# First MLP in blocks of 288 and 432 columns, with six weight chunks streamed and seven more attention slots

## Chip, cores and metric

One core of one Trainium2 chip. The metric is the device time of one execution of the whole program, in microseconds (us). The kernel before took 1003.7 us (median of 3 runs, 1002.4 to 1004.23).

## The reference, cut to what matters

```python
def phi(x):                       # x: 4 batches, 8 heads, 576 positions, 64 deep
    proj = einsum('bhsd,df->bhsf', x, w_phi)          # 128 features
    proj = proj - max(abs(proj), axis=-1)
    return concatenate([exp(proj), exp(-proj)], -1)   # 256
q_p, k_p = phi(q), phi(k)
kv  = einsum('bhsf,bhsd->bhfd', k_p, v);  z = sum(k_p, axis=2)
x   = einsum('bhsf,bhfd->bhsd', q_p, kv) / (einsum('bhsf,bhf->bhs', q_p, z) + 1e-6)
x   = x as (2304 tokens, 512)
h   = x @ w_in1;  x2 = (h * sigmoid(h)) @ w_out1      # 512 -> 2048 -> 512, first MLP
h   = max(x2 @ w_in2, 0);  out = (h * h) @ w_out2     # second MLP
```

All of it is float32 in and out. The weights of both MLPs are float64 in DRAM.

## The kernel before

**Number format.** A float32 value is split into two float32r values, hi (a cast on ACT) and lo (a subtraction on DVE), and a product is three matmuls: lo x hi, hi x lo, hi x hi. So every operand of PE needs one ACT and one DVE operation first (`hi_act` L355, `lo_on` L358; DVE's subtractions all show as L360, ACT's casts as L356).

**Attention.** There are 4 batches j of 576 tokens; 8 heads are handled in pairs, p = 0 to 3. `keys_of(j, p)` (L621) builds phi(k) and kv for one pair of one batch. `queries_of(b, p)` (L863) handles one *half*: b = 0 to 7, 288 tokens, half b belongs to batch b // 2. It projects the queries (L900, L901), takes the maximum over partitions on GpSimd (L911), makes exponentials, splits them, multiplies by kv (L963) and divides: the denominator row goes to DRAM and back in three small DMAs (rr<-qn L978, rd<-rr L985, qb<-rd L988), because the reciprocal is taken with the row spread over 96 partitions. The product x (L1001, two DVE operations) is split into the x buffer of its half. Attention's tiles live in slots of 128 x 576 float32: 28 early ones for batch 0's keys and half 0, 12 (`NT`) for all else; a unit (one pair) can only be under way if one of `NU` = 4 tokens is free.

**First MLP.** 8 blocks of 288 tokens (half b is block b), each with 16 chunk steps; a step (`chunk`, L1019) handles 128 of the 2048 inner columns: 12 matmuls of 288 columns into a PSUM bank (L1035), tanh and gate on ACT and DVE, split, and 12 matmuls that accumulate into four banks (L1071). The 16 weight chunks (8 KB per partition each, hi and lo of both matrices) are converted from float64 once, during block 0 and before (`w_conv` L454, `w_split` L522), and stay in SBUF: 8 tiles in pool `w`, 8 in `wq`, which opens once the early slots are done. The result of a block goes to DRAM (x2d, L1090). I call the steps by number: step 16 i + c is chunk c of block i, 0 to 127.

**Second MLP.** Its weights are converted in 32 parts while the first MLP runs and stored to DRAM (w2d, L546). Its first matrix is multiplied by a seven-product scheme on 2 x 2 sub-blocks (`x_sums` L1098, `w_sums` L552, `quad` L1167, matmuls L1191), the gated result goes to DRAM in 144 KB pieces (gd, L1250), and its second matrix is multiplied in blocks of 512 columns, the last 256 (`gate_of`, `down`, L1294).

**What sets the order.** All operations are listed with an engine, a cost, a key, reads, writes and buffers. `Plan.run` (L160) simulates the engines: whenever an engine is free it takes the ready operation with the lowest key whose buffers are free. The order found so is emitted as the program; on the chip each engine runs its own list in order and waits on semaphores. Keys are chunk steps: the first MLP's step has its own number, and `want` (L1323) places attention at so many steps ahead (the table `KEYS`, L271). All DMAs are issued by SP, in the planned order; a DMA that waits holds up those behind it. There are 8 PSUM banks: four accumulators, two for L1035, two for attention.

**Lines the change touches.** `KEYS` and the `want` calls (L1332 to L1374), the pools (L293 to L336), `w_tile` (L508), `w_split`, `w_sums`, `x_buf` (L856) and the end of `queries_of` (L996 to L1014), `chunk`, `x_sums`, `quad`, `gate_of`, `down`.

Of the kernel before, what the change touches and what calls it, by code (L numbers as in the profile page):

```python
# [51 lines left out]
class Buf:  # L52


    def __init__(self, pool, make, unit):
        self.pool, self.make, self.unit, self.users, self.tile = pool, make, unit, 0, None
# [10 lines left out]
class Plan:  # L67
# [92 lines left out]
    def run(self):  # L160
# [9 lines left out]
        while left:  # L170
            moved = True
            while moved:
                moved = False
                for e in engines:
# [43 lines left out]
            while events and events[0][0] <= now:  # L218
# [45 lines left out]
def dma(kb):  # L264
# [10 lines left out]
    "nwr": 4, "wsp": -6.82,  # L275
# [4 lines left out]
def attention_then_two_mlps(ctx, tc, kT, qT, v, w_phi, w1, w2, out):  # L280
# [9 lines left out]
    NXT, NGQ = 7, 7  # L290
# [4 lines left out]
    xp = ctx.enter_context(tc.tile_pool(name="xp", bufs=2, side="right"))  # L295
    gp = ctx.enter_context(tc.tile_pool(name="gp", bufs=NG, side="right"))
# [20 lines left out]
    def wide_pool():  # L317
# [7 lines left out]
    gd = tc.dram_tile([128, NC, NTOK], F32, name="gd")  # L325
    rd = tc.dram_tile([2 * B * NP, 2 * HB], F32, name="rd")

    plan = Plan({
        "t": NT, "raw": NRAW, "att": NATT, "h": 2, "acc": 0, "eb": 4, "e": NE, "eunits": NEU, "w": NC - NW, "wq": 0, "x": 2, "kv": NP, "v": 2,
        "g": NG, "o": 2, "xx": 2, "rr": 2, "mx": 4, "units": NU, "c": NCV, "xt": 0, "gq": 0, "pb": 0,  # L330
    })
    wide = [0, {"xt": NXT, "gq": NGQ}]
    plan.last = {
        "eb": [0, {"acc": 4}], "e": [0, {"wq": NW}], "t": wide, "kv": wide, "v": wide,
# [4 lines left out]
    def slot(name, unit, shape=(128, S), dt=F32):  # L339
        if unit.early:  # L340
            return Buf("e", lambda: ep[0].tile(list(shape), dt, tag="t", name=name), unit)
        return Buf("t", lambda: tp.tile(list(shape), dt, tag="t", name=name), unit)

    def bank(name, unit, pool_="att"):
        if pool_ == "att" and unit.early == 2:
            pool_ = "eb"
        return Buf(pool_, lambda: psb.tile([128, 512], F32, tag="b", name=name), unit)

# [105 lines left out]
    def w_conv(layer, c, parts, key):  # L454
# [42 lines left out]
        hold = min(int(key) - 6, NB * NC - 1) if layer else 0  # L497
# [24 lines left out]
    def w_split(layer, c, parts, f, u, key, engine):  # L522
# [28 lines left out]

    def w_sums(q, key):  # L552
        u = plan.unit()
        hi, lo = (w_tile(1, 2 * q + x) for x in range(2))
# [9 lines left out]
        def parts(x):  # L564
            return get((hi, lo)[x]).rearrange("p a n -> p (a n)")[:, :7 * 256].rearrange("p (a n) -> p a n", n=256)

        SPLITS = ((0, 2, 0), (3, 4, 2), (0, 4, 3))

        def split_hi(i):
            a, b, o = SPLITS[i]  # L570
            hi_act(parts(0)[:, o:o + b - a], get(f)[:, a:b])

        def split_lo(i):
            a, b, o = SPLITS[i]
            lo_on("DVE", parts(1)[:, o:o + b - a], get(f)[:, a:b], parts(0)[:, o:o + b - a])
# [19 lines left out]
        op(key, "ACT", act(1024), lambda: split_hi(2), r=[(W, 1)], w=[(W, "hi", 2)], bufs=[f, hi], unit=u)  # L595
        op(key, "DVE", dve(1024), lambda: split_lo(2), r=[(W, 1), (W, "hi", 2)], w=[(W, "lo", 2)],
           bufs=[f, hi, lo], unit=u)

# [257 lines left out]
    def x_buf(u):  # L856
        if u not in xs:
            xs[u] = Buf(
                "x", lambda: [xp.tile([128, ND, HB], F32R, tag=f"x{i}", name=f"x{i}_{u}") for i in range(2)], None
            )  # L860
        return xs[u]

    def queries_of(b, p, key, lo_engine="DVE"):  # L863
# [132 lines left out]
        x = Buf("xx", lambda: sp.tile([128, HB], F32, tag="xx", name="x" + n), None)  # L996
        xb = x_buf(b)
# [15 lines left out]
        op(key, "ACT", act(HB), x_hi, r=[(Q, "x")], w=[("xh", b, p)], bufs=[x, xb])  # L1013
        op(key, "DVE", dve(HB), x_lo, r=[(Q, "x"), ("xh", b, p)], w=[("xl", b, p)], bufs=[x, xb])  # L1014
# [4 lines left out]
    def chunk(i, c, key):  # L1019
        n = f"{i}_{c}"  # L1020
        C = ("c", 0, i, c)
        w = wch[0, c]
        xb = xs[i]
        ps = bank("h" + n, None, "h")
        gb = Buf("g", lambda: [gp.tile([128, HB], dt, tag=t, name=t + n)
                               for t, dt in (("a", F32), ("gh", F32R), ("gl", F32R))], None)

        def gemm1():
# [3 lines left out]
            for cc in range(ND):  # L1032
                f = slice(cc * 128, (cc + 1) * 128)
                for a, x in ((ww[:, 1, f], xh), (ww[:, 0, f], xl), (ww[:, 0, f], xh)):
                    nc.tensor.matmul(get(ps)[:, :HB], a, x[:, cc], start=k == 0, stop=k == 3 * ND - 1)  # L1035
                    k += 1

        def f1():
            nc.scalar.activation(out=get(gb)[0], in_=get(ps)[:, :HB], func=AF.Tanh, scale=0.5)  # L1039

        def f2():
            a = get(gb)[0]
            nc.vector.scalar_tensor_tensor(  # L1043
                out=a, in0=a, scalar=1.0, in1=get(ps)[:, :HB], op0=ALU.add, op1=ALU.mult
            )
# [12 lines left out]
        op(key, "ACT", act(HB), g_hi, r=[(C, "g")], w=[(C, "gh")], bufs=[gb])
        op(key, "DVE", dve(HB), g_lo, r=[(C, "g"), (C, "gh")], w=[(C, "gl")], bufs=[gb])
        W = [(("wf", 0, c, 1), "hi"), (("wf", 0, c, 1), "lo")]  # L1060
        for d in range(ND):
# [4 lines left out]
            def gemm2(d=d, acc=acc):  # L1066
# [8 lines left out]
            op(key + P["g2"], "PE", 3 * MM, gemm2, r=W + [(C, "gh"), (C, "gl")], w=[("acc", i, d)],  # L1075
# [349 lines left out]
```

## Time and profile before

| | |
|---|---|
| runs | 1002.4, 1003.7, 1004.23 us |
| profiled execution | 1002.71 us, span 1000.9 us |
| PE busy | 981.7 us (98%), 6656 matmuls |
| DVE, ACT, GpSimd busy | 677.7, 579.5, 94.6 us |
| mean granted TensorE clock | 0.993 |
| DMA | 126.68 MB, mean 127 GB/s |

The span runs from the first to the last instruction; the rest of the execution's time lies around it. "Granted clock" 1.00 is 2.4 GHz, 0.5 is 1.2 GHz; a value between is a mean over a stretch. Matmuls overlap: the bar of one is longer than the distance to the next, so a count of bars in a window has about two more than the window holds, and a busy PE can still be slower than its best. A row of a view of groups reads: line, engine, operation, tile written <- tiles read, shapes, count | busy us, mean ns of one | idle time of the engine ahead of it, and what ended it.

### The profile page before, as it was taken

To read this page: it belongs to the slowest core of one execution; us is meant where nothing else is said; L and a number is where in the kernel's file an instruction comes from. 1 tells how busy PE (TensorE), PEld (TensorE's weight loads), DVE (VectorE), ACT (ScalarE), POOL (GpSimd) and SP (SyncE) were. 2 spreads that over 40 slices of the span, in tenths; PEclk is the share of its full clock that TensorE was granted. 3 is DMA by queue.
4 is the path that set the end of the run, shared out by engine and by line. 5 is a ranking of instruction groups with operands and counts; after the bars stand their busy time and mean duration, and the time that the engine had idled before them with its cause. 6 is when DMAs were issued, how large, how long until landed. Compare 5 with 4: busy or idle time off the path is not lost.

```text
span 1000.9 us, 17956 instructions
## 1 busy us (share of the span) xinstructions
PE 981.7 (98%) x6656; PEld 920.4 (92%) x6656; DVE 677.7 (68%) x1295; ACT 579.5 (58%) x1385; POOL 94.6 (9%) x68
## 2 busy tenths in 40 slices
PE   9969999999999999999999999999999999999998
PEld 6739999999999999999989999999999988888888
DVE  5999997766557777788898799975767733232321
ACT  6867866776777676776574464564555732222221
POOL 3140003210011300011020002010200000000000
PEclk9979999999999999999999999999999999999999
DMA  9536601231102132454545635443436654343322
GB/s 272 175 118 216 217 27 37 61 87 50 39 25 61 44 104 97 135 174 133 139 137 172 209 120 193 166 155 113 148 108 225 205 184 127 103 128 103 119 66 73
DMA packets 76578, 126.68 MB, mean 127 GB/s; under 512 B 14922, under 2 KB 42186, under 8 KB 74442
## 3 DMA queue, kind: packets, MB, share of 16 engines
q1 hardware_dynamic: 76490, 125.54, 40.0%
q8 instruction: 52, 0.85, 0.4%
q14 instruction: 36, 0.29, 0.1%
HBM read 88.64 MB, written 36.79 MB: 125 GB/s over the span
## 4 chain that ended last, share of the span: by engine, by line
PE 93%; DVE 4%; DMA 1%; issue 1%; ACT 0%; POOL 0%; SPq 0%; DVEq 0%
PE h L1035 20%; PE y L1294 20%; PE o L1071 19%; PE pb L1191 7%; PE pc L1191 5%; PE pa L1191 5%; PE pn L963 5%; PE pk L704 3%; PE pkv L766 3%; PE pkv L812 3%; DVE w L360 1%; PE pq L900 1%; PE pq L901 1%; DVE wc L492 1%; DVE wc L488 1%
## 5 line engine op out<-in xcount | busy, mean ns | idle before, releaser
L1071 PE MATMUL o<-gh,w 128*128 128x288 f32 x1024 | 232.1, 298 | 0.0
L1035 PE MATMUL h<-x,w 128*128 128x288 f32 x1536 | 225.1, 296 | 0.1
L1035 PEld LDWEIGHTS h<-x,w 128*128 128x128 f32 x1536 | 211.4, 188 | 1.0 <-ACT mx L726 0.4
L1294 PE MATMUL y<-g,w 128*128 128x512 f32 (+1 forms) x960 | 201.7, 372 | 0.0
L1294 PEld LDWEIGHTS y<-g,w 128*128 128x128 f32 x960 | 167.5, 188 | 33.6
L1071 PEld LDWEIGHTS o<-gh,w 128*128 128x128 f32 x1024 | 172.7, 188 | 2.6 <-issue 1.9
L1071 PE MATMUL o<-gl,w 128*128 128x288 f32 x512 | 150.4, 294 | 0.0
L360 DVE TENSOR_TENSOR g<-gr,g 128x512 fp32r<-128x512 f32 (+1 forms) x80 | 51.0, 638 | 130.3 <-ACT g L356 130.2
L356 ACT CAST g<-gr 128x512 fp32r<-128x512 f32 (+1 forms) x80 | 45.9, 577 | 137.1 <-PE y L1294 134.7
L1039 ACT ACTIVATE a<-h 128x288 f32<-128x288 f32 x128 | 52.9, 413 | 82.3 <-PE h L1035 81.4
L911 POOL PARTITION_ALL_REDUCE qm<-qp x32 | 73.1, 2310 | 257.9 <-ACT qp L904 238.5
L1071 PEld LDWEIGHTS o<-gl,w 128*128 128x128 f32 x512 | 96.4, 188 | 0.2
L1191 PE MATMUL pb<-xt,w 128*128 128x288 f32 x576 | 88.4, 296 | 0.7 <-DVE glq L1206 0.6
L1043 DVE SCALAR_TENSOR_TENSOR a<-a,h 128x288 f32<-128x288 f32 x128 | 57.5, 450 | 43.7 <-ACT a L1039 42.8
L1191 PEld LDWEIGHTS pb<-xt,w 128*128 128x128 f32 x576 | 80.6, 188 | 1.4 <-DVE glq L1206 0.8
L360 DVE TENSOR_TENSOR gl<-a,gh 128x288 fp32r<-128x288 f32 x128 | 64.2, 502 | 11.8 <-ACT gh L356 10.8
L356 ACT CAST gh<-a 128x288 fp32r<-128x288 f32 x128 | 55.9, 437 | 18.5 <-DVE a L1043 18.3
L1191 PE MATMUL pa<-xt,w 128*128 128x288 f32 x384 | 60.9, 296 | 0.4 <-ACT aq L1213 0.4
L1191 PE MATMUL pc<-xt,w 128*128 128x288 f32 x384 | 61.1, 295 | 0.0
L1191 PEld LDWEIGHTS pa<-xt,w 128*128 128x128 f32 x384 | 54.4, 188 | 0.9 <-ACT aq L1213 0.9
L1191 PEld LDWEIGHTS pc<-xt,w 128*128 128x128 f32 x384 | 54.6, 188 | 0.3 <-DVE g L1206 0.2
L1243 ACT ACTIVATE g<-g 128x288 f32<-128x288 f32 x64 | 28.0, 438 | 31.7 <-DVE g L1206 31.7
(119 smaller groups left out, 1521.4 us busy)
## 6 DMA issues: line engine op xcount, KB each, us to landing
gd<-g SPq DMA_DIRECT2D x128, 144.0 KB, 1.8
wbits<-w SPq DMA_DIRECT2D x16, 1024.0 KB, 5.5
wr<-w SPq DMA_DIRECT2D x32, 512.0 KB, 4.4
gr<-gd SPq DMA_DIRECT2D x32, 512.0 KB, 3.7
w2d<-wc SPq DMA_DIRECT2D x32, 256.0 KB, 3.5
qr<-qT SPq DMA_DIRECT2D x56, 144.0 KB, 3.1
v<-v SPq DMA_DIRECT2D x16, 325.0 KB, 3.8
kr<-kT SPq DMA_DIRECT2D x16, 288.0 KB, 3.8
```

The source lines that it names most:

```text
L356: nc.scalar.copy(out=dst, in_=src)
L360: e.tensor_tensor(out=dst, in0=src, in1=hi.bitcast(F32), op=ALU.subtract)
L704: nc.tensor.matmul(o, get(kk)[:, ks], ww.rearrange("p a f -> p (a f)"), start=x == 0, stop=x == len(ops) - 1)
L766: nc.tensor.matmul(get(pkv)[:D1, a * 256:(a + 1) * 256], w, y, start=t == 0 and a == 0 and x == 0, stop=t == NKT - 1 and x == 2, skip_grou ...
L911: nc.gpsimd.partition_all_reduce(get(mx), get(pr).rearrange("p a t -> p (a t)"), 128, bass.bass_isa.ReduceOp.absmax)
L963: nc.tensor.matmul(get(ps)[:D1, :HB], w, get(e)[:, t], start=x == 0, stop=x == len(ops) - 1)
L1035: nc.tensor.matmul(get(ps)[:, :HB], a, x[:, cc], start=k == 0, stop=k == 3 * ND - 1)
L1039: nc.scalar.activation(out=get(gb)[0], in_=get(ps)[:, :HB], func=AF.Tanh, scale=0.5)
L1043: nc.vector.scalar_tensor_tensor(out=a, in0=a, scalar=1.0, in1=get(ps)[:, :HB], op0=ALU.add, op1=ALU.mult)
L1071: nc.tensor.matmul(get(acc)[:, :HB], a, g, start=c == 0 and x == 0, stop=c == NC - 1 and x == 2)
L1191: nc.tensor.matmul(get(ps)[:, :HB], wpart(a, prod)[:, f], x[:, y, cc], start=first and k == 0, stop=k == 5, skip_group_check=True,)
L1294: nc.tensor.matmul(get(acc)[:, :cols], ww[:, c % 2 * 2 + a, f], g[:, y, :cols], start=c == 0 and x == 0, stop=c == NC - 1 and x == 2,)
```

## The change

The first MLP gets six blocks, two of 288 and four of 432 columns, in place of eight of 288. A block's x buffer collects the halves or parts of halves that fall into it (`pieces`). Six of the sixteen weight chunks (1, 4, 7, 9, 12, 14) no longer stay in SBUF: after their conversion they are stored to DRAM (w1d), and are loaded again for each later block (`w_again`), the load waiting for the step of the streamed chunk but one before it. Pool `wq` shrinks from 8 tiles to 4. The memory goes into seven more slots (`NTL`) and two more unit tokens (`NUL`) for attention, which open with `wq`, into wider x, g and y buffers, and later into tiles of the second MLP. The second MLP's gate results are stored in pieces of 288 KB, two halves at once; of its first matrix, the lo parts for q = 3 and 7 are spread over the unused eighths of other tiles. The keys of attention and of the weight conversions are given anew.

```diff
+WIDTHS = (288, 288, 432, 432, 432, 432)
+STARTS = [sum(WIDTHS[:i]) for i in range(len(WIDTHS))]
+NL, LB = len(WIDTHS), max(WIDTHS)
+STREAM = (1, 4, 7, 9, 12, 14)
+IN_W = (0, 1, 2, 3, 4, 5, 6, 7, 11, 13, 15)
+SPREAD = (3, 7)
+def pieces(b):
+    return [
+        (i, max(b * HB, at), min(b * HB + HB, at + n))
+        for i, (at, n) in enumerate(zip(STARTS, WIDTHS)) if at < b * HB + HB and b * HB < at + n
+    ]
+def key_of(i, c=0):
+    return NC * STARTS[i] / HB + c * WIDTHS[i] / HB
...
-    "k0s": 13.54, "q0s": 11.97, "q0": 5.97, "w0": 42.81, "ws": 4.4, "we": 0.61, "q1": 20.14, "qo": 18.1,
-    "qs": 0.24, "k1": 34.92, "k": 26.62, "ks": 0.3, "qe": 3.1, "w2a": 53.0, "w2b": 1.6, "bx": 3, "pe": 49.5,
-    "el": 219.23, "wl": 4.53, "kl": 3.21, "vl": -27.16, "ql": 7.48, "phl": 1.63, "g2": 2.23, "phi": 13.71,
-    "nwr": 4, "wsp": -6.82,
+    "k0s": 13.54, "q0s": 16.25, "q0": 5.97, "w0": 42.81, "ws": 4.4, "we": 0.61, "Q1": -4.1, "A1": -0.68,
+    "Q2": 17.0, "Q3": 19.0, "A2": 29.74, "Q4": 42.0, "Q5": 61.0, "A3": 60.97, "Q6": 66.0, "Q7": 91.57,
+    "qs": 0.24, "ks": -0.73, "w2a": 66.58, "w2b": 2.2, "bx": 3, "pe": 49.5, "el": 219.23, "wl": 3.86,
+    "kl": 3.21, "vl": -27.16, "ql": 7.48, "phl": 1.63, "g2": 2.23, "phi": 13.71, "nwr": 4, "wsp": -7.5,
+    "sw": 22.81, "ss": 6,
...
+    NWQ, NTL, NUL = 4, 7, 2
...
-        "eb": [0, {"acc": 4}], "e": [0, {"wq": NW}], "t": wide, "kv": wide, "v": wide,
+        "o": [0, {"gq": 1}], "eb": [0, {"acc": 4}], "e": [0, {"wq": NWQ, "x1": 1, "xy": 1, "gl": 1, "t": NTL, "units": NUL}], "t": opened, "kv": opened, "v": opened,
...
+    def x_pair(i, shape, dt, name):
+        k = i % 2
...
+        return Buf(f"x{k}", make, None)
...
+        if layer == 0 and c in STREAM:
+            def keep():
+                nc.sync.dma_start(out=w1d[STREAM.index(c)], in_=get(w).bitcast(F32).rearrange("p a n -> p (a n)"))
+
+            op(key, "SP", dma(1024), keep, r=[(("wf", 0, c, x), t) for x in parts for t in ("hi", "lo")], w=[("w1d", c)],
+               bufs=[w])
+
+    def w_again(i, c, key):
+        w = w_tile(0, c, i)
+
+        def load():
+            nc.sync.dma_start(out=get(w).bitcast(F32).rearrange("p a n -> p (a n)"), in_=w1d[STREAM.index(c)])
+
+        k = STREAM.index(c)
+        before = (("c", 0, i if k > 1 else i - 1, STREAM[k - 2]), "h")
+        op(key, "SP", dma(1024), load, r=[("w1d", c), before], w=[("w", i, c)], bufs=[w])
...
+        late = b > 0 and p % 2
+        x = Buf(
+            "xy" if late else "xx",
+            lambda: (late_pool() if late else sp).tile([128, HB], F32, tag="xx", bufs=1 if late else 2, name="x" + n), None
+        )
...
+        for i, s0, s1 in pieces(b):
+            xb = x_buf(i)
+            here, there = slice(s0 - b * HB, s1 - b * HB), slice(s0 - STARTS[i], s1 - STARTS[i])
...
+            op(key, "ACT", act(s1 - s0), x_hi, r=[(Q, "x")], w=[("xh", i, b, p)], bufs=[x, xb])
+            op(key, "DVE", dve(s1 - s0), x_lo, r=[(Q, "x"), ("xh", i, b, p)], w=[("xl", i, b, p)], bufs=[x, xb])
...
-                    nc.tensor.matmul(get(ps)[:, :HB], a, x[:, cc], start=k == 0, stop=k == 3 * ND - 1)
+                    nc.tensor.matmul(get(ps)[:, :cols], a, x[:, cc, :cols], start=k == 0, stop=k == 3 * ND - 1)
...
-                        get(acc)[:, :HB], a, g, start=c == 0 and x == 0, stop=c == NC - 1 and x == 2
+                        get(acc)[:, :cols], a, g[:, :cols], start=c == 0 and x == 0, stop=c == NC - 1 and x == 2
...
-            want(t + 16 - P["q1" if j == 0 else "qo"] + P["qs"] * p, queries_of, 2 * j + 1, p)
+            want(P[f"Q{2 * j + 1}"] + P["qs"] * p, queries_of, 2 * j + 1, p)
             if j + 1 < B:
-                want(t + 32 - P["k1" if j == 0 else "k"] + P["ks"] * p, keys_of, j + 1, p)
-                want(t + 32 - P["qe"] + P["qs"] * p, queries_of, 2 * j + 2, p)
-    base2 = 16 * NB
+                want(P[f"A{j + 1}"] + P["ks"] * p, keys_of, j + 1, p)
+                want(P[f"Q{2 * j + 2}"] + P["qs"] * p, queries_of, 2 * j + 2, p)
+    base2 = NC * NB
+    for i in range(1, NL):
+        for c in STREAM:
+            at = key_of(i, c) - 0.5
+            want(at, "key", lambda key, i=i, c=c: w_again(i, c, key - P["sw"]), at)
```

In the changed kernel the keys are still counted in steps of 288 columns, so block 2 begins at step 32, block 3 at 56, block 4 at 80 and block 5 at 104. Block 2 takes half 2 and the first part of half 3, block 3 the rest of half 3 and half 4, block 4 half 5 and the first part of half 6, block 5 the rest of half 6 and half 7.

## Rows read from the trace of the kernel before

**Rows 1.** Part 1 of the page: busy time of each engine.
```profile
PE 981.7 (98%) x6656; PEld 920.4 (92%) x6656; DVE 677.7 (68%) x1295; ACT 579.5 (58%) x1385; POOL 94.6 (9%) x68
```

**Rows 2.** Part 4 of the page: the chain that ended last, by line.
```profile
PE h L1035 20%; PE y L1294 20%; PE o L1071 19%; PE pb L1191 7%; PE pc L1191 5%; PE pa L1191 5%; PE pn L963 5%; PE pk L704 3%; PE pkv L766 3%; PE pkv L812 3%; DVE w L360 1%; PE pq L900 1%; PE pq L901 1%; DVE wc L492 1%; DVE wc L488 1%
```

**Rows 3.** Windows: length, PE, PEld, DVE, ACT, POOL busy (count), clock, DMA share, GB/s.
```profile
0.00:74.00 74.00, 62.17 (x305) 43.95 (x305) 58.25 (x91) 52.33 (x116) 21.11 (x20) 0.93 0.60 190
74.00:150.00 76.00, 76.00 (x553) 71.96 (x552) 70.89 (x114) 58.00 (x156) 0.68 (x4) 1.00 0.46 153
220.00:490.00 270.00, 270.00 (x2072) 267.25 (x2071) 193.88 (x382) 194.54 (x520) 26.73 (x18) 1.00 0.30 89
490.00:510.00 20.00, 17.35 (x119) 16.64 (x118) 16.35 (x32) 11.71 (x27) 3.45 (x2) 0.91 0.65 173
606.00:634.00 28.00, 26.88 (x193) 25.54 (x192) 26.38 (x51) 15.00 (x33) 6.46 (x4) 1.00 0.67 222
```

**Rows 4.** Windows of steady matmuls: 288 columns, 512 (L1294 alone), 256 (PE alone).
```profile
535.00:585.00 50.00, 50.00 (x378) 50.00 (x378) 41.98 (x90) 24.31 (x55) 0.00 (x0) 1.00 0.56 175
...
800.00:950.00 150.00, 150.00 (x647) 121.66 (x646) 1.00 0.42 129
...
982.00:996.00 14.00, 14.00 (x120) 1.00 0.01 3
```

**Rows 5.** Groups by line: the first MLP's matmuls.
```profile
L1071 PE MATMUL o<-gh,w 128*128 128x288 f32 x1024 | 232.1, 298 | 0.0
L1035 PE MATMUL h<-x,w 128*128 128x288 f32 x1536 | 225.1, 296 | 0.1
...
L1071 PE MATMUL o<-gl,w 128*128 128x288 f32 x512 | 150.4, 294 | 0.0
```

**Rows 6.** Groups by line and shape: ACT and DVE of a chunk step, and 512 columns.
```profile
L356 ACT CAST gh<-a 128x288 fp32r<-128x288 f32 x128 | 55.9, 437 | 18.5 <-DVE a L1043 18.3
L1039 ACT ACTIVATE a<-h 128x288 f32<-128x288 f32 x128 | 52.9, 413 | 82.3 <-PE h L1035 81.4
...
L360 DVE TENSOR_TENSOR gl<-a,gh 128x288 fp32r<-128x288 f32 x128 | 64.2, 502 | 11.8 <-ACT gh L356 10.8 <-PE pn L963 0.2
L1043 DVE SCALAR_TENSOR_TENSOR a<-a,h 128x288 f32<-128x288 f32 x128 | 57.5, 450 | 43.7 <-ACT a L1039 42.8
...
L360 DVE TENSOR_TENSOR g<-gr,g 128x512 fp32r<-128x512 f32 x60 | 41.5, 692 | 107.7 <-ACT g L356 107.7
```

**Rows 7.** Issue to landing: the 1 MB weight loads (wbits), then rr and rd hops.
```profile
DMA to landing us min/median/max: 4.9/5.5/14.4
...
DMA to landing us min/median/max: 1.4/2.0/5.2
```

**Rows 8.** Instructions of a line: duration, first and last start; last row a window of L1035.
```profile
L1001 DVE TENSOR_TENSOR x<-qn,qb x16: 440/451/453, 172.7 to 227.5; 64x288 f32<-64x288 f32 x16
...
L1035 PE MATMUL h<-x,w x9: 288/295/298, 220.9 to 222.0; 128*128 128x288 f32 x9
...
L1001 DVE TENSOR_TENSOR x<-qn,qb x8: 409/452/454, 476.4 to 502.1; 64x288 f32<-64x288 f32 x8
...
L1035 PE MATMUL h<-x,w x24: 292/295/297, 421.6 to 430.2; 128*128 128x288 f32 x24
...
L766 PE MATMUL pkv<-kh,vl x40: 276/280/335, 374.6 to 444.1; 128*65 128x256 f32 x32, 64*65 64x256 f32 x8
...
220.00:490.00 270.00, 109.05 (x745) 102.38 (x746) 1.00 0.30 89
```

**Rows 9.** Chain from 491 to 502 (start, us, what), and PE's timeline after it.
```profile
491.22 2.62 DMA rr<-qn
...
494.28 3.88 DMA rd<-rr
...
498.23 3.40 DMA qb<-rd
...
503.41 0.50 PE L963 MATMUL pn<-qo,kv 128*65 128x288 f32 x1 [2.28 <-DVE qo L360]
```

More of the change, by code (lines that the diff above doesn't have):

```diff
@@ L55, in __init__ @@
     def __init__(self, pool, make, unit):
[L56 removed]
+        self.pool, self.make, self.unit, self.users, self.tile, self.home = pool, make, unit, 0, None, None
 class Unit:
@@ L76, in __init__ @@
         self.last = {}
+        self.homes = {p: list(range(32)) for p in ("t", "xt", "gq")}
     def unit(self):
@@ L550, in attention_then_two_mlps, with w_at, w_runs @@
     SLOT = {1: 0, 2: 1, 4: 2, 6: 3, 3: 4, 7: 5, 5: 6}
+    def w_at(layer, q, x, slot):
+        if q not in SPREAD or x == 0:
+            return w_tile(layer, 2 * q + x), slot
+        if slot == 0:
+            return w_tile(layer, 2 * q), 7
+        return w_tile(layer, 2 * (q - 3) + slot - 1), 7
+    def w_runs(layer, q, x, at, n):
+        runs = []
+        for i in range(n):
+            b, s = w_at(layer, q, x, at + i)
+            if runs and runs[-1][0] is b and runs[-1][1] + runs[-1][3] == s:
+                runs[-1][3] += 1
+            else:
+                runs.append([b, s, i, 1])
+        return runs
     def w_sums(q, key):
         u = plan.unit()
-        hi, lo = (w_tile(1, 2 * q + x) for x in range(2))
+        hi, lo = ([b for b, *_ in w_runs(1, q, x, 0, 7)] for x in range(2))
         f = Buf("raw", lambda: rp.tile([128, 4, 256], F32, tag="raw", name=f"ws{q}"), None)
@@ L854, in attention_then_two_mlps, with x_buf @@
     xs = {}
[L856 to L861, printed above, removed]
+    def x_buf(i):
+        if i not in xs:
+            xs[i] = x_pair(i, (128, ND, LB), F32R, f"x_{i}")
+        return xs[i]
     def queries_of(b, p, key, lo_engine="DVE"):
@@ L1060, in chunk @@
-        W = [(("wf", 0, c, 1), "hi"), (("wf", 0, c, 1), "lo")]
+            lo_on("DVE", get(gb)[2][:, :cols], get(gb)[0][:, :cols], get(gb)[1][:, :cols])
+        again = c in STREAM and i > 0
+        W = [("w", i, c)] if again else [(("wf", 0, c, 0), "hi"), (("wf", 0, c, 0), "lo")]
+        halves = [b for b in range(NB) if any(x[0] == i for x in pieces(b))]
+        op(key, "PE", 3 * ND * (13 + cols / 2.4), gemm1, r=W + [(t, i, b, p) for t in ("xh", "xl") for b in halves for p in range(NP)],
+           w=[(C, "h"), "order"], bufs=[ps, w, xb])
@@ L1061, in chunk @@
+        op(key, "ACT", act(cols, True), f1, r=[(C, "h")], w=[(C, "a")], bufs=[ps, gb])
+        op(key, "DVE", dve(cols), f2, r=[(C, "a")], w=[(C, "g")], bufs=[ps, gb])
+        op(key, "ACT", act(cols), g_hi, r=[(C, "g")], w=[(C, "gh")], bufs=[gb])
+        op(key, "DVE", dve(cols), g_lo, r=[(C, "g"), (C, "gh")], w=[(C, "gl")], bufs=[gb])
+        if not again:
+            W = [(("wf", 0, c, 1), "hi"), (("wf", 0, c, 1), "lo")]
         for d in range(ND):
@@ L1100, in x_sums @@
         u = plan.unit()
-        own = Buf("x", lambda: [xp.tile([128, 2, 2, HB], F32, tag=f"x{k}", name=f"xr{k}_{s}") for k in range(2)], None)
-        new = own if s == 0 else Buf(
-            "x", lambda: [xp.tile([128, 2, 2, HB], F32, tag=f"x{k}", name=f"xs{k}_{s}") for k in range(2)], None
-        )
+        own = x_pair(s and 1, (128, 2, 2, HB), F32, f"xr_{s}")
+        new = own if s == 0 else x_pair(0, (128, 2, 2, HB), F32, f"xs_{s}")
         X = ("xr", s)
@@ L1301, in down @@
             return
-        yb = Buf("x", lambda: [xp.tile([128, 2, 512], F32, tag=f"x{k}", name=f"y{k}_{i}") for k in range(2)], None)
+        yb = x_pair(i, (128, 2, 512), F32, f"y_{i}")
         for d in range(ND):
@@ L1371, in attention_then_two_mlps @@
             want(key, "key", lambda key, i=i, c=c: gate_of(i, c, key), key)
-    for i in range(NB):
+    for i in range(NL):
         for c in range(NC):
-            want(16 * i + c, "chunk", i, c)
+            want(key_of(i, c), "chunk", i, c)
     for _, _, key, f, args in sorted(todo, key=lambda x: x[:2]):
```

223 lines of the change are left out of this document (132 added, 91 removed).

## The prediction

> **What bounds the kernel now.** I read the page first: PE is busy 98% of the 1000.9 us span [rows 1], and the chain that ended last lies on PE for 93%, with the two matmul lines of the first MLP (L1035, L1071) at 20% and 19% [rows 2]. So the time is PE's own work plus the few stretches in which PE lacks work, and a change counts by matmuls removed or stalls made. By stage [rows 3], PE is full from 74 to 150 and from 220 to 490. It lacks work before 74 (62.17 of 74 us busy, granted clock 0.93), loses a little at 490 to 510 (17.35 of 20, clock 0.91) and at 606 to 634 (26.88 of 28). Busy is not pace, so I took the pace from steady stretches [rows 4]. About two bars hang over each window's start (a bar is some 295 ns, its pace 133), so: 288 columns 50/376 = 133.0 ns, 512 columns 150/645 = 232.6 ns, 256 columns 14/118 = 118.6 ns. A straight line through 256 and 512 is 4.6 ns + 0.445 ns a column and gives 132.8 at 288, which was measured as 133.0: the fixed part of a matmul is small.
>
> **The change, part by part.**
>
> *Wider blocks.* The first MLP issues 1536 + 1024 + 512 = 3072 matmuls of 288 columns [rows 5], 384 a block. Two blocks stay; the other six (2304 matmuls) become four of 432 (1536). The columns are the same, 768 matmuls go. By the line 432 columns take 4.6 + 0.445 x 432 = 196.8 ns: 2304 x 133.0 = 306.4 us become 1536 x 196.8 = 302.3 us, **-4.1 us**. No row has 432. If the 144 columns beyond 288 ran at the full clock, 60.0 ns, it would be 193.0 ns and -10.0 us; 232.6 less 80 columns at the full clock is 199.3 ns and -0.3 us. I take the line, since it met its third point.
> The Trainium skill (TensorE: Matmul & The Clock Gate, Back-to-back issue gap) gives a warm gap of N/2.4 + 2.5 ns, by which 768 matmuls fewer would be worth 1.9 us and the forecast 2.2 us higher. By that rule 288 columns would take 122.5 ns; the trace, at 133.0 ns, does not agree.
>
> *ACT and DVE.* A chunk's two DVE operations of 450 and 502 ns and two ACT ones of 413 and 437 ns [rows 6] are done 96 times instead of 128, wider. They lie beside PE; some 9 us of DVE are freed (450 ns at 288 and 692 at 512 columns [rows 6] make about 605 at 432, and 2 x (96 x 0.450 - 64 x 0.605) = 9.0). I cost this at nothing; what covers it is PE being full. Splitting halves 3 and 6 over two blocks adds 8 short casts and 8 short subtractions, also nothing.
>
> *Six streamed chunks.* Added on SP's queue: 6 stores and 30 loads of 1 MB. A 1 MB load lands in 5.5 us at the median, 14.4 at worst, issue to landing [rows 7]. Two slots rotate, so a load has the distance between a chunk and the next but one of its kind: 5 or 6 chunks, one of them spent on finishing the old one. That is at least 4 x 24 x 133 ns = 12.8 us in a 288 block, 18.9 in a 432 block. Over 5.5, so nothing; if the worst case came each time in block 1, 1.6 us each for six loads, 10 us at most. The 64 gate stores saved on SP (128 become 64) come later and don't matter. What is queued behind a load that waits for its slot on SP: attention's loads, its three hops for the reciprocal (rr, rd, qb), the second MLP's conversions and x2d's stores. 31.5 MB over some 450 us is 70 GB/s on top of the 89 between 220 and 490 [rows 3].
>
> *More attention slots, earlier due dates.* 12 slots become 19 and 4 units 6 after the start. A 432 block needs more of the attention at once: half 3 is due at chunk step 32 instead of 48, half 6 at 80 instead of 96, half 7 at 104 instead of 112. Half 3 is no problem: halves 2 and 3 were multiplied out by 227.5, and block 2 started at 220.9 [rows 8]; half 3's 64 matmuls on PE (8.5 us) move ahead of it to 229. Half 6 is: it was done at 502, and PE reached step 80 at 421.6 [rows 8]. What PE still had to do for it after 421.6 now lies ahead of step 80: a third of the 120 kv matmuls of keys 3 (they run from 374.6 to 444.1 [rows 8]) and some projections, about 50 at 118.6 ns or 6 us, and half 6's 8.5 us; 2 us are saved. PE gets there at 434. So what took from 220 to 502 must fit into 220 to 434. Work for it: from 220 to 490 DVE is busy 193.9 us and ACT 194.5 [rows 3], of which 62 chunk steps (745 bars of L1035 less two, 12 a step [rows 8]) are 59 and 53; 48 steps' worth at the new width is 46 and 41. So 181 and 183 us of 214, **85% and 86%**, against 72% now. Throughput must grow 282/214 = 1.32 times, slots grow 1.58 times and units 1.5 times: I take it that it fits, at nothing, without much room. Bounds: 0 if it fits; with the throughput of 12 slots half 6 would be 68 us late.
> At block starts 2 and 4 there is a further tail: the pair p=3 of halves 3 and 6 waits for the buffer of p=1, which waits for the other x buffer, held by the block just ending: two casts, two subtractions and a multiplication, about 0.44 + 0.45 + 0.9 + 0.44 + 0.45 = 2.7 us. The held-back second matmuls of two chunks, 2 x 2.36 us, cover it.
>
> *The stall at 490 to 510.* 119 - 2 matmuls in 20 us is 15.6 us of work, so 4.4 us are lost. The chain shows how [rows 9]: three DMA hops of 2.62, 3.88 and 3.40 us, DVE standing in order behind the last, PE waiting 2.28 us for a qo queued on DVE, then a granted clock of 0.91 over these 20 us, with the DMA engines at 0.65 [rows 3]. In the new order these instructions stand elsewhere: 4.4 taken away. Of the four later block starts only 2 and 4 have a half due just then; I charge each 1.3 us, the middle between nothing and the 2.65 us idle here (bounds for all four: 0 and 17.6, four whole stalls). Net **-1.8 us**.
>
> *Start and seam.* Before 74 half 0's units are only spread otherwise; 6 MB of stores join a DMA share of 0.60. Bounds -3 to +3, taken 0. At 606 to 634 DVE is busy 26.38 of 28 [rows 3]; conversions of w2 begin earlier but are spread wider and end later (step 129.6 against 124.6), and the spread weight pieces add 8 subtractions of some 0.4 us: +0.5 (0 to +3).
>
> **Sum.** -4.1 - 1.8 + 0.5 = -5.4. The profiled execution took 1002.7 us (span 1000.9 plus 1.8 around it) and becomes 997.3; the median of the runs, 1003.7, stands 1.0 above it, so I forecast **998.3 us**.
>
> **Rivals.**
> *It gains more.* 432 columns at 193.0 ns and no new stall: -10.0 - 4.4 = -14.4, 989.3 us. For: only three widths were seen. Against: they lie on one line.
> *What is won is lost again at the block starts.* Each later start pays 1 to 2 us while the in-order DVE and SP queues stand behind late hops: +5.4 in all, 1003.7. For: that is what the one stall in the middle was, and DMA traffic grows. Against: PE from 220 to 490 had none [rows 3].
> The Trainium skill (DMA: Bandwidth & Descriptors, Queues, rings and completion order) says that each DMA engine takes one queue's descriptors in ring order, so a 2 KB hop stands behind a 1 MB load. The trace agrees in size: hops land in 2.0 us at the median and 5.2 at worst [rows 7].
> *Slower: half 6 comes late to block 4.* One place, step 80. If throughput grows 1.25 times where 1.32 are needed, half 6 takes 282/1.25 = 226 us, 12 us too long. PE idles 12 us and loses clock after it, 1.8 us if as at 490 to 510 (20 us at 0.91 [rows 3]): 998.3 + 13.8 = 1012.1. It decides from 5.4 us late on, where it has eaten the gain. For: 85% on two engines that feed each other. Against: DVE was busy 70.89 of 76 us from 74 to 150 and PE stayed full [rows 3].
>
> **How the numbers follow.** Forecast 0.50, gains more 0.12, lost again 0.14, slower 0.24. A measurement tells 0.2% (2.0 us) from nothing: faster is below 1001.7, slower above 1005.7. Faster 0.50 + 0.12 = 0.62, same 0.14, slower 0.24. The matmul's bounds alone spread the forecast from 992.4 to 1002.1; the range goes on to 989 for the first rival and over the second to 1010, most of the way to the last, which leaves out some 0.18.
>
> **What would show it.** In the profile after: L1035 and L1071 with 768 matmuls of 288 columns and 1536 of 432, at 196 to 198 ns in a steady stretch; no wait of PE for the streamed tile's load; DVE and ACT above 80% between 220 and 440; the idle of PE at 490 to 510 gone and the first gemm of block 4 directly behind block 3's last. It is wrong if 432 columns take over 199 or under 194 ns, if PE waits more than 5 us before block 2 or 4 for x, or if the clock drops in mid-run.

## The result and the profile after

| | before | after |
|---|---|---|
| median of the runs | 1003.14 us (1002.4 to 1004.23, 4 runs) | 995.06 us (993.76 to 996.24, 4 runs) |
| profiled execution | 1002.71 us | 994.13 us |
| its span, mean granted clock | 1000.9 us, 0.993 | 992.4 us, 0.995 |

The ratio of after to before is 0.9918, with a 95% interval of 0.9900 to 0.9937: faster by 8.1 us, where 5.4 was forecast. The time lies inside the predicted range.

First the busy time of each engine, and the chain that ended last by line (the kernel after; answers to [rows 1, 2]):

```profile
PE 974.0 (98%) x5888; PEld 898.9 (91%) x5888; DVE 674.8 (68%) x1243; ACT 569.1 (57%) x1325; POOL 97.5 (10%) x68
...
PE y L1413 20%; PE o L1188 19%; PE h L1149 19%; PE pb L1305 8%; PE pc L1305 5%; PE pa L1305 5%; PE pn L1070 3%; PE pk L813 3%; PE pkv L875 3%; PE pkv L921 3%; DVE w L430 1%; DMA rr<-qn 1%; PE pq L1007 1%; DVE x L1111 1%; PE pq L1008 1%
```

PE has 768 matmuls fewer and is still the bound at 98%. The groups of L1149 and L1188, which were L1035 and L1071 [rows 5], by shape (busy us, mean ns, then the idle before them):

```profile
L1149 PE MATMUL h<-x,w 128*128 128x432 f32 x768 | 159.7, 358 | 0.0
L1188 PE MATMUL o<-gh,w 128*128 128x432 f32 x512 | 157.0, 360 | 0.0
L1188 PE MATMUL o<-gl,w 128*128 128x432 f32 x256 | 92.1, 360 | 0.0
L1188 PE MATMUL o<-gh,w 128*128 128x288 f32 x256 | 59.0, 299 | 0.0
L1149 PE MATMUL h<-x,w 128*128 128x288 f32 x384 | 57.4, 298 | 2.3 <-DVE x L430 1.7 <-ACT x L426 0.5 <-DVE w L430 0.2
L1188 PE MATMUL o<-gl,w 128*128 128x288 f32 x128 | 38.2, 298 | 1.5 <-DVE gl L430 1.4
```

These are 1536 matmuls of 432 columns and 768 of 288, as announced. The 432 groups stand with no idle time before them; the little there is falls in block 0. The means are durations that overlap, so the pace is read from a steady window. The windows of the kernel after (columns as in [rows 3]):

```profile
0.00:68.00 68.00, 59.39 (x305) 42.62 (x305) 55.21 (x84) 50.98 (x113) 22.70 (x20) 0.95 0.68 220
68.00:150.00 82.00, 78.18 (x555) 72.50 (x554) 77.51 (x122) 63.37 (x165) 5.56 (x6) 1.00 0.62 217
220.00:434.00 214.00, 213.94 (x1311) 203.58 (x1310) 158.81 (x284) 168.52 (x430) 32.89 (x18) 1.00 0.44 138
430.00:460.00 30.00, 29.96 (x163) 28.44 (x162) 26.93 (x59) 20.76 (x47) 4.76 (x2) 1.00 0.68 211
490.00:510.00 20.00, 20.00 (x104) 19.18 (x103) 13.53 (x26) 7.18 (x13) 0.00 (x0) 1.00 0.65 203
535.00:595.00 60.00, 60.00 (x308) 57.58 (x307) 48.34 (x94) 27.94 (x51) 0.00 (x0) 1.00 0.62 210
595.00:625.00 30.00, 27.70 (x173) 26.88 (x172) 27.56 (x50) 14.03 (x29) 6.19 (x4) 0.94 0.61 196
```

- 535 to 595 holds nothing but L1149 and L1188 at 432 columns: 60/306 = 196.1 ns each, two bars taken off as in [rows 4].
- The stall at 490 to 510 is gone: PE 20.00 of 20, clock 1.00, where it was 17.35 at 0.91.
- Step 80 (448.4 us, below) lies in a window in which PE is busy 29.96 of 30.
- The first gemm starts at 68.0 instead of 73.9, but the stretch after it, which was full, now has 3.8 us of idle. Step 16 begins at 153.6 against 152.7: the sooner start is given back.
- At the seam to the second MLP (595 to 625) there is more idle than before, with a clock of 0.94 where 606 to 634 had 1.00.

All that PE waits for, by releaser (total us, times, longest):

```profile
PE pn L1070 <- ACT qe L1036: 6.3, 3, 5.5
PE pb L1305 <- DVE glq L1320: 2.3, 1, 2.3
PE warm L514 <- ACT zeros L479: 2.3, 1, 2.3
PE h L1149 <- DVE x L430: 1.7, 2, 0.8
PE o L1188 <- DVE gl L430: 1.4, 2, 1.1
PE h L1149 <- ACT x L426: 0.5, 1, 0.5
PE h L1149 <- DVE w L430: 0.2, 1, 0.2
```

No line names the streamed tile's load. In the list of DMA issues (KB each, median us to landing) it stands as

```profile
w<-w1d SPq DMA_DIRECT2D x30, 1024.0 KB, 5.3
```

with a worst landing of 8.4 us, under the 12.8 us that a load has. The pn wait, and all of L1149's and L1188's, lie in the first 150 us; pn's was 9.6 us there. What has grown after that is pb's wait for glq, at the seam: 2.3 us, where it was 0.6. The chain shows what held glq (kernel after; start us, us, what):

```profile
604.46 0.43 DVE ws L688
...
604.92 1.55 DVE ws L688
...
606.49 1.55 DVE ws L688
...
608.07 1.50 DVE ws L688
609.57 0.38 DVE glq L1320
...
609.99 1.50 PE pb L1305 x6
```

and this is GpSimd's timeline beside it:

```profile
604.46 1.72 POOL L1259 TENSOR_TENSOR xs<-xr 128x576 f32<-128x576 f32 x1 [1.44 <-DMA xr<-x2d]
...
606.13 1.61 POOL L1259 TENSOR_TENSOR xs<-xr,xs 128x576 f32<-128x576 f32 x1
607.83 1.46 POOL L1259 TENSOR_TENSOR xs<-xr,xs 128x576 f32<-128x576 f32 x1
```

GpSimd's three operations on x2d (L1259) end at 606.18, 607.74 and 609.29. The last three of DVE's four sums of weight pieces (L688) take 1.5 us each and end at 606.47, 608.04 and 609.57: each ends 0.3 us after one of GpSimd's. The first, which starts together with GpSimd's first, takes its usual 0.43. Alone an L688 takes 425 ns, its median over the run; before, its counterpart L578 never took more than 427. glq stands behind them in DVE's order, and PE behind glq.

### The profile page after: what moved, and what is told of

It is laid out like the page before. It is cut to its first block, busy times and chain, and to the rows that moved or that the text cites. A ratio compares the mean times of both kernels' runs of the same rounds, so it can differ in the third digit from the quotient of the medians.

```text
span 992.4 us, 16130 instructions
## 1 busy us (share of the span) xinstructions
PE 974.0 (98%) x5888; PEld 898.9 (91%) x5888; DVE 674.8 (68%) x1243; ACT 569.1 (57%) x1325; POOL 97.5 (10%) x68
## 4 chain that ended last, share of the span: by engine, by line
PE 91%; DVE 5%; ACT 2%; DMA 1%; issue 1%; POOL 0%; ACTq 0%; POOLq 0%; DVEq 0%
PE y L1413 20%; PE o L1188 19%; PE h L1149 19%; PE pb L1305 8%; PE pc L1305 5%; PE pa L1305 5%; PE pn L1070 3%; PE pk L813 3%; PE pkv L875 3%; PE pkv L921 3%; DVE w L430 1%; DMA rr<-qn 1%; PE pq L1007 1%; DVE x L1111 1%; PE pq L1008 1%
## 5 line engine op out<-in xcount | busy, mean ns | idle before, releaser
L1149 PE MATMUL h<-x,w 128*128 128x432 f32 (+1 forms) x1152 | 217.0, 338 | 2.3 <-DVE x L430 1.7
L1188 PE MATMUL o<-gh,w 128*128 128x432 f32 (+1 forms) x768 | 216.0, 340 | 0.0
L1149 PEld LDWEIGHTS h<-x,w 128*128 128x128 f32 x1152 | 196.7, 188 | 9.8 <-DVE x L430 2.1
L1188 PEld LDWEIGHTS o<-gh,w 128*128 128x128 f32 x768 | 140.2, 189 | 5.6 <-issue 1.7
L1188 PE MATMUL o<-gl,w 128*128 128x432 f32 (+1 forms) x384 | 130.4, 339 | 1.5 <-DVE gl L430 1.4
L1413 PE MATMUL y<-g_0h,w 128*128 128x512 f32 (+1 forms) x320 | 98.4, 372 | 0.0
L1413 PE MATMUL y<-g_1h,w 128*128 128x512 f32 (+1 forms) x320 | 98.0, 372 | 0.0
L1188 PEld LDWEIGHTS o<-gl,w 128*128 128x128 f32 x384 | 72.3, 188 | 4.0 <-DVE gl L430 2.2
L1413 PEld LDWEIGHTS y<-g_1h,w 128*128 128x128 f32 x320 | 58.5, 188 | 11.4
L1413 PEld LDWEIGHTS y<-g_0h,w 128*128 128x128 f32 x320 | 58.5, 188 | 11.3
L430 DVE TENSOR_TENSOR gl<-a,gh 128x432 fp32r<-128x432 f32 (+1 forms) x96 | 57.3, 597 | 14.6 <-ACT gh L426 13.7
L1413 PE MATMUL y<-g_1l,w 128*128 128x512 f32 (+1 forms) x160 | 59.5, 372 | 0.0
L1413 PE MATMUL y<-g_0l,w 128*128 128x512 f32 (+1 forms) x160 | 59.5, 372 | 0.0
```

What stands on the lines that cost most here:

```text
L430: e.tensor_tensor(out=dst, in0=src, in1=hi.bitcast(F32), op=ALU.subtract)
L1149: nc.tensor.matmul(get(ps)[:, :cols], a, x[:, cc, :cols], start=k == 0, stop=k == 3 * ND - 1)
L1188: nc.tensor.matmul(get(acc)[:, :cols], a, g[:, :cols], start=c == 0 and x == 0, stop=c == NC - 1 and x == 2)
L1413: nc.tensor.matmul(get(acc)[:, :cols], ww[:, c % 2 * 2 + a, f], g[y][:, :cols], start=c == 0 and x == 0, stop=c == NC - 1 and x == 2,)
```

## The experiments

**The seam: GpSimd's sums later.** Theory: DVE is held up by GpSimd, so if GpSimd's second group starts after DVE's crowded stretch, the wait goes. The edit lets the load of that group wait for a product of the first quad step:

```diff
+        deps += [(("q", 0, 4), "p4")] if s == 1 else []
```

> The load behind the second MLP's sums for s = 1 waits for quad 4 of s = 0, so that GpSimd's four subtractions come some 25 us later; nothing else is changed. Theory: in the changed kernel PE waits 2.30 us at the seam for a DVE addition, because four DVE subtractions of 425 ns ahead of it took 5.11 us together, three of them some 1.55 us each while GpSimd's subtractions ran from 604.46 to 609.28; apart in time, both run at their usual length, the wait goes and the clock does not fall, 2 to 4 us less than the changed kernel: 991 to 993 us. Rival (the slow DVE operations come from something else, such as DMA writes): the wait stays, 995 us.

989.95 us (988.91 to 990.34), 0.9872 of before [0.9857, 0.9887]. GpSimd's group now starts at 637.4, no L688 takes more than 427 ns, and PE is full over the same window:

```profile
595.00:625.00 30.00, 30.00 (x203) 29.58 (x203) 27.84 (x61) 17.36 (x37) 0.00 (x0) 1.00 0.57 193
```

The ratio falls by 0.0046, 4.6 us, a little over what was expected: besides the wait, the clock of 0.94 and slow DVE operations go. The edit moves the load of x2d along with the sums; that the sums are what held DVE up is read from the ends of the operations above, not separated by a run.

**The same in the kernel before.** The same line added to it.

> The kernel before with one wait more: the load behind the second MLP's sums for s = 1 comes after quad 4 of s = 0. Theory: the seam of the kernel before loses 2.7 us in the same way (DVE operations of 0.69 us took 1.9 and 1.2 us while GpSimd subtracted from 612.39 to 619.65); apart in time, 1.5 to 3 us shorter, 999.5 to 1001 us. Rival (in the kernel before DVE had time left there, PE's longest wait being 0.57 us): no change, 1002 to 1003 us.

1000.6 us (999.37 to 1001.94), 0.9977 [0.9966, 0.9988]: 2.3 us, so before had this loss too, at half the size. Its stall near 500 stays (PE waits 2.7 us for a qo of DVE).

**Only the order, in the kernel before.** Eight blocks of 288 and 12 slots as they were, the late sums, and five keys chosen anew (the keys between them left out):

```diff
-    ... "k": 26.62, ... "qe": 3.1, "w2a": 53.0, ... "pe": 49.5, ... "wl": 4.53, ...
+    ... "k": 25.49, ... "qe": 4.72, "w2a": 60.17, ... "pe": 46.98, ... "wl": 4.81, ...
```

> The kernel before with the late sums and with seven of its keys chosen again (k, qe, w2a, pe, wl and others by some steps), so that the order at 490 to 510 is another one. Theory: the 4.4 us lost there are a matter of the order alone and not of widths or slots; together with the seam 5 to 7 us shorter than the kernel before, 995.5 to 998 us. Rival (with 12 slots half 6 cannot be in time, whatever the order): PE still waits 2 us or more there, 1000 us or more.

995.97 us (995.12 to 997.08), 0.9929 [0.9917, 0.9942]. The whole list of PE's waits is

```profile
PE pn L963 <- ACT qe L929: 9.9, 2, 5.1
PE warm L444 <- ACT zeros L409: 2.3, 1, 2.3
```

So the stall at 490 to 510 was a matter of order. It needed neither wider blocks nor slots, and without them this kernel is 7.1 us faster: 2.3 by the late sums and 4.8 by the keys (0.9929 against 0.9977). Against the first experiment, which has the new layout and no such waits either, it is 0.0057 or 5.7 us slower: that is what the layout, the wide blocks with the streaming and slots that they need, brings by itself.

**The wide blocks away.** The kernel after, streaming and slots kept, in eight blocks of 288 with 42 loads, keys chosen anew:

```diff
-WIDTHS = (288, 288, 432, 432, 432, 432)
+WIDTHS = (288,) * 8
```

> The changed kernel with eight blocks of 288 columns; streaming (now 42 loads), slots, layout stay, and attention's and the conversions' keys are chosen again for the old due dates. Theory: the changed kernel's gain is first of all its 768 fewer matmuls (2304 at 133 ns against 1536 at 196 ns, 5.5 us); without them the same layout is at least 5.5 us slower than the changed kernel, 1000 to 1008 us, that is no faster than the kernel before. Rival (slots and the new order of attention bring the gain, the widths none): 993 to 997 us.

1005.15 us (1004.32 to 1006.59), 1.0021 [1.0011, 1.0031]. In this order streaming and slots alone bring nothing. It is 10 us behind the kernel after, more than the matmul term; its order has waits of its own, 4.2 us at the seam among them, so what streaming and slots cost without the widths is not separated. Here a streamed load does hold PE, once, for 1.0 us (`PE h L1149 <- DMA w<-w1d: 1.0, 1, 1.0`).

**A matmul's cost, by doubling their number.** The 432-column matmuls of the first gemm are done as two of 216 columns, 768 more, with the same weights and result:

```diff
+                    for n in (slice(0, 216), slice(216, 432)) if cols == 432 else (slice(0, cols),):
+                        nc.tensor.matmul(get(ps)[:, n], a, x[:, cc, n], ...)
```

> Each of the 768 matmuls of 432 columns of the first MLP's first product is done as two of 216 columns, so 768 more matmuls with the same columns. Theory (the straight line of the prediction, 4.6 ns + 0.445 ns a column): two of 216 take 201.4 ns where one of 432 took 196.0, 4.1 us longer in all, 999 us. Rival (a matmul with its own weight load has a floor near the 118.6 ns of 256 columns): two take some 237 ns, 31 us longer, 1026 us.

1016.6 us (1014.26 to 1017.3), 1.0135 [1.012, 1.015], 21.5 us above the kernel after: 28 ns for each matmul added. Here are the window 535 to 595 of this kernel, all lines, then L1150 (216 columns) and L1192 (432) alone (PE, PEld, clock, DMA share, GB/s):

```profile
535.00:595.00 60.00, 60.00 (x430) 58.82 (x430) 41.30 (x76) 25.81 (x47) 0.00 (x0) 1.00 0.69 229
...
535.00:595.00 60.00, 33.27 (x286) 33.30 (x286) 1.00 0.69 229
...
535.00:595.00 60.00, 30.00 (x144) 26.33 (x144) 1.00 0.69 229
```

With 144 matmuls at 196.1 ns, 286 are left with 31.8 us, 111 ns each. The straight line of the prediction gives 100.7 and was expected to hold; 118.6, as at 256 columns, was the other value. It is neither: the line does not go on below 256 columns. PE is full in this window, so this is pace and not waiting.

**The slots away.** The kernel after without its seven slots and two units:

```diff
-        ... "e": [0, {"wq": NWQ, "x1": 1, "xy": 1, "gl": 1, "t": NTL, "units": NUL}], ...
+        ... "e": [0, {"wq": NWQ, "x1": 1, "xy": 1, "gl": 1}], ...
```

> The seven late slots and the two more unit tokens are not given to attention; widths, streaming and keys stay. Theory: the wide blocks need the slots, because half 6 has to be done some 65 us sooner than in the kernel before and 12 slots give its old pace; block 4 starts late, PE idles there and the time is 40 to 70 us longer, 1035 to 1065 us. Rival (the slots only fill memory that came free, and attention has room without them): under 5 us longer, at most 1000 us.

1043.14 us (one run), 40 us slower than before. So that its order is not to blame, the same with keys chosen anew:

> The changed kernel without the seven slots and two tokens, with its keys chosen again for that. Theory: what 12 slots lack is throughput of attention between steps 32 and 80, so another order only spreads the loss: still 15 to 40 us longer than the changed kernel, 1010 to 1035 us. Rival (the 48 us of the run without new keys were mostly a bad order): under 8 us longer, at most 1003 us.

1018.79 us (one run), still 15 us slower than before. PE around step 80, in the first and then in the second of these kernels (windows):

```profile
425.00:475.00 50.00, 40.56 (x223) 35.55 (x222) 33.01 (x56) 37.44 (x100) 8.07 (x5) 0.83 0.41 127
```

```profile
425.00:475.00 50.00, 32.24 (x170) 25.83 (x169) 35.12 (x62) 35.69 (x90) 13.25 (x6) 0.81 0.34 96
```

No engine is busy over 82% there, and the clock falls as well, to 0.83 and 0.81. Step 80 starts at 497.7 and at 476.9 us, where the kernel after has 448.4, and in both within 0.7 us of the end of half 6's last split. This is the rival "half 6 comes late to block 4", and it is what the slots buy off.

**More DMA traffic.** Each streamed load is followed by a copy of the same megabyte within DRAM, which nobody reads. It has no wait of its own:

```diff
+            nc.sync.dma_start(out=w1x[(i - 1) * len(STREAM) + STREAM.index(c)], in_=w1d[STREAM.index(c)])
```

> Behind each of the 30 streamed loads one more DMA of 1 MB is issued that copies the chunk within DRAM, which nobody waits for; the order of all else is the same. Theory: the streamed traffic lies beside PE's work and has room, hops and loads land later by 1 to 2 us at the median, and the time grows by 0 to 3 us, 995 to 998 us. Rival (late hops make the in-order DVE and SP queues stand, and PE with them): 6 to 15 us longer, with PE waits of 1 to 3 us at several block starts.

1004.62 us (1002.23 to 1009.16, 10 runs), 1.0017 [1.0004, 1.0029]: 9.9 us slower than the kernel after by the ratios, so my theory that there was room fell. Its rival held in the size, less in the places: one long wait stands ahead of block 4, shorter ones of 0.8 to 1.6 us inside blocks 1 and 2. The trace is of the slowest of the ten runs. The window 450 to 520 of it, then pieces of its chain (start us, us, what):

```profile
450.00:520.00 70.00, 66.15 (x344) 62.82 (x343) 51.25 (x103) 33.42 (x72) 4.80 (x2) 0.98 0.81 273
```

```profile
438.47 4.36 DMA rr<-qn
...
447.31 10.20 DMA qb<-rd
...
459.43 0.77 DVE ql L431
...
460.24 0.40 PE pq L1009
```

One hop of the reciprocal takes 10.20 us. DVE, in order, reaches ql only after the four x that need it, and PE waits (3.9 us at the longest). Over the rr and rd hops the median landing is 2.7 us and the worst 10.3. It was 2.3 and 8.8 in the kernel after, and 2.0 and 5.2 before [rows 7].

**The start order.** The late-sums kernel with the key q0s put back to its old value (16.25 to 11.97).

> The changed kernel with late sums and the old spacing of half 0's queries (11.97 in place of 16.25 steps). Theory: the first chunk starts 5.9 us sooner in the changed kernel, but step 16 starts no sooner, because DVE's weight conversions set the pace of block 0; so the old spacing changes the time by under 1.5 us, 988.5 to 991.5 us. Rival (the sooner start is part of the gain): 993 to 996 us.

991.33 us (991.14 to 993.08), 0.9881 [0.9865, 0.9898], against 0.9872 [0.9857, 0.9887]: no difference that the intervals tell. The first gemm starts at 68.3 instead of 68.4 us, so this key is not what made it sooner. Step 16 starts at 156.1 instead of 154.0 in these two traces, so up to 2 us there may still hang on the key. Which other key made the first gemm sooner was not tried, since nothing of it is left by step 16.

**Keys chosen by the measured pace.** The late-sums kernel, with the matmul costs by which its order is made set to 4.6 + 0.445 ns a column in place of 13 + columns/2.4, and the keys chosen anew:

```diff
-        op(key, "PE", 3 * ND * (13 + cols / 2.4), gemm1, ...)
+        op(key, "PE", 3 * ND * (4.6 + 0.445 * cols), gemm1, ...)
```

> The changed kernel with the late sums, with a matmul's cost in the planner as measured (4.6 ns + 0.445 ns a column) and with its keys chosen again under it. Theory: nearly all that is left to gain lies ahead of step 16, where PE works 27 us below its pace up to 75 us and 9 us from there to 150; the new keys win 1 to 4 us on the changed kernel with late sums, 986 to 989 us. Rival (what is left there is bound by the chain of the first units and by DVE's weight conversions, whatever the order): 989 to 992 us.

990.99 us (990.83 to 993.06), 0.9883 [0.987, 0.9897]: no gain: the theory missed and its rival held. In the late-sums kernel PE is busy 830.66 of 831 us from 154 to 985, so behind step 16 an order has next to nothing left to win with these matmuls. The lowest median is that of the change with the late sums: 989.95 us, 1.3% under before.

## Why the prediction came out right

**Wider blocks: -4.1 forecast, -5.2 by the pace after.** Right in its mechanism, a little small in its size. 2304 x 133.0 = 306.4 us became 1536 x 196.1 = 301.2 us in the steady window, a gain of 5.2; by the ratio of the two kernels without other waits it is 5.7. 196.1 lies 0.7 ns under the straight line's 196.8 and well off both bounds, 193.0 and 199.3. So interpolating was right. Below the line's points it would have been wrong, by 10 ns at 216 columns. The formula that the prediction quotes from the Trainium skill (TensorE: Matmul & The Clock Gate, Back-to-back issue gap) is given there for a matmul by itself, not for a stream; by it 432 columns would take an estimated 182.5 ns, where this stream took 196.1.

**ACT and DVE at nothing: right.** They hold PE up nowhere between 220 and 595. At 432 columns the four operations of a chunk take (busy us, mean ns):

```profile
L426 ACT CAST gh<-a 128x432 fp32r<-128x432 f32 x64 | 35.6, 557 | 15.1 <-DVE a L1157 14.7
L1153 ACT ACTIVATE a<-h 128x432 f32<-128x432 f32 x64 | 33.9, 532 | 71.0 <-PE h L1149 71.0
...
L430 DVE TENSOR_TENSOR gl<-a,gh 128x432 fp32r<-128x432 f32 x64 | 40.9, 640 | 11.6 <-ACT gh L426 11.3
L1157 DVE SCALAR_TENSOR_TENSOR a<-a,h 128x432 f32<-128x432 f32 x64 | 38.3, 600 | 36.9 <-ACT a L1153 36.4
```

600 ns answers to the 605 that I had worked out from [rows 6].

**Streaming at nothing: right for PE, and with less room than I gave it.** The loads were never late. What is queued behind them on SP was the weaker side: the hops grew from 2.0 to 2.3 us at the median, and the copies of the experiment turned that into 9.9 us. The Trainium skill (DMA: Bandwidth & Descriptors, Queues, rings and completion order) says that one queue's descriptors are taken in ring order; the hop of 10.20 us agrees with a hop that stands behind megabytes, though no run here moved the hops to another queue. The second rival was thus a real mechanism, but not at the traffic of this change.

**Attention in time: right in its outcome, with two readings wrong.** The first is the load. I had DVE at 181 and ACT at 183 of 214 us, 85% and 86%. The 46 and 41 us in it are 48 chunk steps at the old width; at the new one they are 32 steps, by the means above 32 x (640 + 600) ns = 39.7 us and 32 x (557 + 532) ns = 34.8 us, which makes about 175 and 176 us in all. The second is the place: 421.6 us is not the start of step 80 in the kernel before. Between the start of step 32 and 421.6 lie 552 matmuls of L1035, 46 steps of 12, so step 78 starts there, and step 80 at 432.20. The kernel before (L1035 alone: PE, PEld, clock, DMA share, GB/s; then PE's timeline), and a window of the kernel after, all engines:

```profile
220.90:421.60 200.70, 80.90 (x552) 75.80 (x553) 1.00 0.24 71
...
432.20 1.76 PE L1035 MATMUL h<-x,w 128*128 128x288 f32 x12
```

```profile
220.00:448.40 228.40, 228.31 (x1388) 217.04 (x1387) 171.44 (x312) 177.55 (x452) 32.89 (x18) 1.00 0.46 146
```

In the kernel after, PE came to step 80 at 448.4 us, not at 434. Of these 14.4 us the misreading makes 10.6. Some 3.2 more are half 7's first pair, 24 matmuls that I had not counted: between the start of block 2 and step 80 stand 156 of pn and 60 of pq, where halves 4, 5 and 6 have 144 and 48. DVE and ACT were busy 171.44 and 177.55 us up to there, 75% and 78% of 228.4, so the sign "above 80%" did not come. The throughput had to grow 282/228 = 1.24 times, not 1.32; the 1.25 of the last rival's example would have been in time.

That block 2 started at 229.4, where I had 229, is luck. I moved half 3's matmuls ahead of it, but they stood ahead of it in the kernel before too: 160 of pn had started by then in both kernels. What came ahead of it instead were 52 more matmuls of keys (pk, pkv, pkt) and 21 more of L1188.

There was little to spare. DVE's timeline, then PE's, at step 80 of the kernel after:

```profile
444.43 1.86 DVE L1111 TENSOR_TENSOR x<-qn,qb 64x288 f32<-64x288 f32 x4 [0.85 <-DMA qb<-rd]
...
447.11 0.97 DVE L430 TENSOR_TENSOR x<-x,x 128x144 fp32r<-128x144 f32 x4
...
448.17 0.35 PE L1188 MATMUL o<-gh,w 128*128 128x432 f32 x1
448.36 0.95 PE L1149 MATMUL h<-x,w 128*128 128x432 f32 x4
```

Half 6's last part is ready at 448.1, and PE takes it at 448.4 without a gap. The rival that this half comes late was near: the kernels with 12 slots show it happen, so its chance of 0.24 does not look too high.

**The stall at 490 to 510: -4.4 taken away, and it went.** But I gave the gain to the change, and the old layout gets it too from five keys, 4.8 us by the ratios. It belongs to the new order, not to blocks or slots.

**A new tail at block starts 2 and 4: 2.6 charged, not paid.** This term failed. The work held back covered the tail, as I had argued one paragraph earlier myself: no wait stands there, and the window around block 4 is full but for 0.04 us.

**The seam: +0.5 forecast, about +2.3.** The other term that failed, inside its bounds of 0 to +3. The late sums win 4.6 us in the kernel after and 2.3 in the one before, so the seam costs about 2.3 more now; the intervals of these ratios reach 1 to 2 us to either side, so the size is rough. I had counted more DVE work there, not that some of its operations stand still while GpSimd works.

**The start at nothing: right.** 5.9 us sooner, given back by step 16, which starts 0.9 us later than before.

Summed as measured: -5.2 - 4.4 + 2.3 = -7.3 of the 8.1 us of the medians; 0.8 us are not assigned, less than these sizes are known to. The forecast was 2.7 us short: 2.6 charged at the block starts and not paid, and 1.1 more from the matmuls, less 1.8 more at the seam, and this 0.8. That it came so near is in part luck: two failed terms pull in opposite directions.

## What to carry to other kernels

A change that comes with a new order should be split in two: the old layout with its order chosen anew, and the new layout without waits. Here the order with the late sums gave 7.1 us without the layout, and the layout by itself 5.7 us. Count the instructions of the engine that is the bound, at a pace interpolated between measured sizes, and do not carry the line on outside them. Where a queue carries both megabytes and short hops in a chain that an in-order engine waits for, look at the hops' worst landing before adding traffic, not at the large loads' own slack. When a step is looked up in a trace by its time, count its matmuls from a known step: two steps missed moved a due time here by 10.6 us.

## What the runs showed of the hardware that I had not expected

- **DVE beside GpSimd.** A DVE operation with both inputs in SBUF went from 0.43 to 1.55 us at the seam, its end tied to the end of a GpSimd operation. One with an input from PSUM was not held up: in the kernel before, GpSimd is at work from 615.96 to 619.65 (one row of its timeline), and between two slow ones of wc, 1.91 and 1.17 us where 0.69 is usual, glq keeps its 0.44 us (DVE timeline):

```profile
614.63 1.91 DVE L488 SCALAR_TENSOR_TENSOR wc<-wr,wc 128x512 int32<-128x512 int32 x1
616.47 0.45 DVE L1230 TENSOR_TENSOR g<-pa,g 128x288 f32<-128x288 f32 x1
616.84 0.44 DVE L1206 TENSOR_TENSOR glq<-pb,aq 128x288 f32<-128x288 f32 x1
617.20 1.17 DVE L492 SCALAR_TENSOR_TENSOR wc<-wr,wc 128x512 int32<-128x512 int32 x1
```

The Trainium skill (SBUF — State Buffer, SBUF: two separate sides) states that the two engines share a pair of ports under an exclusive lock held for a whole instruction, and that a DVE operation with two SBUF inputs competes for it with a GpSimd one that reads SBUF. The trace agrees, on which operations wait and on how long: 1.55 us, where one of GpSimd's takes 1.46 to 1.72.

- **Short matmuls.** 216 columns took 111 ns, 256 take 118.6, 288 take 133.0 and 432 take 196.1. What sets the lower end was not separated; each of these matmuls loads its own weights.
- **Hops.** A hop of the reciprocal (qb<-rd, 144 KB) took 10.2 us in the queue of the megabyte loads, in a window with a DMA share of 0.81, where its median in that kernel was 4.3.
